# Attention followed by an MLP on one core: scores on half-height row groups side by side, the mask as a factor, two units issued together

## The chip, the cores and the metric

The kernel runs on one core of a Trainium2 chip. The metric is the device time in microseconds (us); for the kernel before, the median of three runs is 324.76 us (324.6 to 324.99). A profiled execution of the same program gives the trace that is read here. The engines are named as in the profile: PE is TensorE (PEld its weight loads), DVE is VectorE, ACT is ScalarE, POOL is GpSimd and SP is SyncE, which here only issues DMAs.

## The reference

The inputs q, k and v have 4 batches, 8 heads, 768 positions and 64 columns per head. The attention is masked by blocks of 32 positions; its output, heads joined to 512 columns, goes through a residual MLP block:

```python
scores = scale * np.matmul(q, k.transpose(0, 1, 3, 2))      # scale = 1/8
mask = np.abs(blk_i - blk_j) <= window                      # blocks of 32, window 1
mask = mask | (blk_i == 0) | (blk_j == 0) | (blk_i == n_blocks - 1) | (blk_j == n_blocks - 1)
...                                                         # and 3 sampled key blocks per query block
scores = np.where(mask, scores, -1000000000.0)
attn = np.exp(scores - max) ; attn = attn / (sum + 1e-09)
x = attn @ v                                                # [4, 768, 512]
a1 = alpha1 * x + beta1
u = x + lam * np.einsum('ts,bsd->btd', w_tok, a1)
out = u + lam * (np.maximum((alpha2 * u + beta2) @ w_ch1, 0.0) @ w_ch2)
```

The mask is the same for all batches and heads. The output is float32.

## The kernel before

**Pairs and units.** The 32 heads are taken as 16 pairs of two heads (`i` from 0 to 15, four pairs per batch). A pair has 12 units `(i, c, j)`: `c` picks one of two halves of 384 queries, `j // 3` the head `w`, and `j % 3` a group `jp` of 256 keys. There are 192 units, and the main loop (line 735) has one step for each of them, and a few more at the end. Positions are laid out so that partition p holds positions 6p to 6p+5; tile `o` of six holds every sixth position.

**A unit.** `emit_qk` (line 310) computes the transposed scores of 256 keys by 384 queries: two matmuls (line 324), one per 128 keys (`jj`), into the two banks of an `sp` tile in PSUM, of which there are two. ScalarE then takes the exponential of both banks in one instruction (line 332) into a tile `eT` in f16. `emit_pv` (line 337) multiplies eT with the values: six matmuls (line 345) per unit, which add up in one `op` tile per `(i, c)`. The values have a column of ones beside them, so the row sums come along. The value matmuls of a unit are issued `LAG` = 2 steps after its scores. With the last of a half, `emit_finish` (lines 360, 362) divides by the sums into `x_sb`, and `emit_a1pp` (lines 376, 377) applies alpha1 and beta1, on POOL for all but the last half of a batch.

**The mask before.** It is added within the score matmul. The contraction has 88 rows: 64 columns of the head and 24 rows that hold, for the queries, which of the 24 blocks a position is in, and for the keys a penalty of -400 (`BIG8`) where the block may not be seen. After the scale of 1/8 and the exponential, such a score leaves nothing.

**How q and k get there.** The loads go over POOL's queue and cast to bf16 (line 111). For pairs 0 to 5, VectorE copies q and k into a joint tile (`emit_lay`, line 126), TensorE transposes (line 267) and VectorE copies out of PSUM into rows 0 to 63 of `qTs`/`kTs` (lines 273, 276). For pairs from 6 (`XP`) on, VectorE copies q and k into the tiles `ql`/`kl`, 128 columns per tile of positions, in which the 24 mask columns already stand (`emit_mask_cols`, line 281, and `emit_mask_spread`, line 290, put them there once); a DMA transpose on SP's queue (`emit_tdma`, line 300) writes `qTs`/`kTs`. These are issued in steps 3 and 4 of the pair before, counted from its first unit.

**What else is in the loop.** The order of the work is written out by hand. For the first steps, `at(s, ...)` puts a piece of work on step s: the copies and transposes of the first pairs, the transposes of w_tok, the loads of the MLP's weights, the first token-mixing jobs. From step 55 (`OPEN`) on, `pour` takes MLP jobs from a queue at a fixed rate of cost per step: `job_tok` (line 485; its result is added on VectorE, lines 500 and 506), the transpose of u (by DMA, line 530, and line 539 on VectorE, or on TensorE, lines 515 and 516), `job_f1` (line 553, with the Relu on ScalarE, line 560) and `job_f2` (line 572, with the residual sum on VectorE, line 581, and the store on SP's queue). What is left of the queue after the last unit runs to the end without attention work. Line 453 multiplies w_ch2 by lam once, at steps 64 to 73. The jobs share three PSUM tiles `mm`; each is free again when its result has been read.

**Within a step** the order is: scores of the unit, loads, copies and DMA transposes for a later pair, jobs, value matmuls of an earlier unit. Each engine works off its own instructions in this order, and so does each DMA queue.

Of the kernel before, what the change touches and what calls it, by code (L numbers as in the profile page):

```python
# [11 lines left out]
FP = mybir.dt.float32  # L12
F16 = mybir.dt.float16
BF = mybir.dt.bfloat16
I32 = mybir.dt.int32
AF = mybir.ActivationFunctionType
ALU = mybir.AluOpType
# [3 lines left out]
S = 768  # L21
D = 64
BLK = 32
NBLK = S // BLK
NR = 3
DM = 512
P = 128
NT = S // P
NH = 4 * DM // P
QC = 384  # L30
NP = H // 2
XP = 6
BIG8 = 400.0
SCALE = 1.0 / 8.0
EXPB = -0.35667494
# [6 lines left out]
def kernel(  # L42
# [16 lines left out]
    nc = tc.nc  # L59
# [3 lines left out]
    indq_np = (tok[None, :] // BLK == np.arange(NBLK)[:, None]).astype(  # L63
        ml_dtypes.bfloat16
    )
# [9 lines left out]
    ms_np = np.concatenate([mstat_np] + [kbi_np] * NR, axis=1)  # L75

    ident_dr = nc.inline_tensor(np.eye(P, dtype=ml_dtypes.bfloat16), name="ident_c")
    indt_np = np.ascontiguousarray(
        indq_np.reshape(NBLK, NT, P).transpose(2, 1, 0).reshape(P, NT * NBLK)
    )  # L80
    indt_dr = nc.inline_tensor(indt_np, name="indt_c")
    indq_dr = nc.inline_tensor(indq_np, name="indq_c")
    ident8_dr = nc.inline_tensor(np.eye(8, dtype=np.float32), name="ident8_c")
    ms_dr = nc.inline_tensor(ms_np, name="ms_c")
# [4 lines left out]
    ap_ = ctx.enter_context(tc.tile_pool(name="attn", bufs=1))  # L89
# [4 lines left out]
    def ptile(shape, dt, name):  # L94
        return pp.tile(shape, dt, name=name, tag=name)
# [6 lines left out]
    raws = {}  # L102
    qks = {}

    def emit_load(i, which="qkv"):
        b, hp = i // NP, i % NP
        for nm, src, dt in (("q", q, BF), ("k", k, BF), ("v", v, F16)):
            if nm not in which or (i, nm) in raws:
                continue
            t = ap_.tile([P, 2, NT * D], dt, name=nm + "r", tag=nm + "r", bufs=2)  # L110
            nc.gpsimd.dma_start(  # L111
                t[:], src[b, 2 * hp : 2 * hp + 2].rearrange("w (p o) d -> p w (o d)", o=NT)
            )
            raws[(i, nm)] = t

    def emit_lay(i, nm, w=slice(0, 2), copy=None):
        raw = raws[(i, nm)][:, w].rearrange("p w (o d) -> p w o d", d=D)
        if nm != "v" and i >= XP:
            dst = (qls if nm == "q" else kls)[i % 2][:, w, :, 0:D]
        elif nm == "v":  # L120
            dst = vexts[i % NVB][:, w, :, 0:D]
        else:
            if i not in qks:
                qks[i] = ap_.tile([P, 2, NT, 2, D], BF, name="qk", tag="qk", bufs=2)
            dst = qks[i][:, w, :, "qk".index(nm), :]
        (copy or nc.vector.tensor_copy)(out=dst, in_=raw)  # L126


    for nm in "qkv":
        raws[(0, nm)] = ap_.tile(  # L130
            [P, 2, NT * D], FP, name=nm + "f", tag="otf_" + nm, bufs=1
        )
    sampi = ptile([P, 2 * NR], I32, "sampi")
    ms = ptile([P, (1 + NR) * NBLK], FP, "ms")
    identb = ptile([P, P], BF, "identb")
    NQB = 4
    qTs = [ptile([P, 2, S], BF, f"qTs{i}") for i in range(NQB // 2)]
    kTs = [ptile([P, 2, S], BF, f"kTs{i}") for i in range(NQB // 2)]
    qText = [qTs[n // 2][:, n % 2] for n in range(NQB)]
    kText = [kTs[n // 2][:, n % 2] for n in range(NQB)]  # L140

    qls = [ptile([P, 2, NT, P], BF, f"ql{i}") for i in range(2)]
    kls = [ptile([P, 2, NT, P], BF, f"kl{i}") for i in range(2)]
    indt = ptile([P, NT, NBLK], BF, "indt")
    maskt = ptile([P, NT, NBLK], BF, "maskt")

    def load_first(nm, src, w, eng):
        eng.dma_start(
# [26 lines left out]
        )  # L175
    for i in range(2, NQB):
        nc.sync.dma_start(qText[i][D : D + NBLK, :], indq_dr.ap())
    nc.sync.dma_start(indt[:], indt_dr.ap().rearrange("p (o n) -> p o n", o=NT))
    warm = ptile([P, DM], BF, "warm")
    nc.vector.memset(warm[:], 0.0)  # L180
    for t in vexts:
        nc.gpsimd.memset(t[:, :, :, D : D + 1], 1.0)
    for t in qls + kls:
        nc.gpsimd.memset(t[:, :, :, D + NBLK : P], 0.0)

    gate = ptile([P, 1], FP, "gate")
    nc.gpsimd.tensor_copy(out=gate[:], in_=raws[(0, "v")][:, 0, 0:1])
# [60 lines left out]
    def mm_tile(shape=(P, DM), dt=FP):  # L248
        return psum.tile(list(shape), dt, name="mm", tag="mm", bufs=3)
# [28 lines left out]
            )  # L278
            qa = qb

    def emit_mask_cols():
        tps = mm_tile((P, NT, NBLK), BF)
        rows = slice(D, D + NBLK)
        for o in range(NT):
            nc.tensor.transpose(
                tps[:, o, :], kText[0][rows, ts(o, P)], identb[rows, rows]
            )
        nc.vector.tensor_copy(out=maskt[:], in_=tps[:])

    def emit_mask_spread():  # L290
        for ts_, src in ((qls, indt), (kls, maskt)):
            for t in ts_:
                nc.gpsimd.tensor_copy(
                    out=t[:, :, :, D : D + NBLK],
                    in_=src[:].unsqueeze(1).broadcast_to([P, 2, NT, NBLK]),
                )

    def emit_tdma(i, nm):
        dst, src = ((qTs, qls) if nm == "q" else (kTs, kls))
        nc.sync.dma_start_transpose(  # L300
            out=dst[i % 2][:].rearrange("p w (o t) -> p (w o) t", t=P),
            in_=src[i % 2][:].rearrange("p w o d -> p (w o d)"),
        )

    ets = {}
    ops = {}
# [3 lines left out]
    def emit_qk(i, c, j, spare=0):  # L310
        w, jp = j // 3, j % 3
        n = (2 * i + w) % NQB
        sp = sp_tile()
        for jj in range(2):
            for _ in range(spare if jj else 0):
                nc.tensor.matmul(
                    sp[:, 0, QC:],
                    warm[:, 0:P],
                    warm[:, 0:P],
                    start=False,  # L320
                    stop=True,
                    skip_group_check=True,
                )
            nc.tensor.matmul(  # L324
                sp[:, jj, 0:QC],
                kText[n][0 : D + NBLK, ts(2 * jp + jj, P)],
                qText[n][0 : D + NBLK, ts(c, QC)],
                start=True,
                stop=True,
            )  # L330
        eT = ap_.tile([P, 2, QC], F16, name="eT", tag="eT", bufs=5)
        nc.scalar.activation(  # L332
            eT[:], sp[:, :, 0:QC], AF.Exp, bias=expb[:], scale=SCALE
        )
        ets[(i, c, j)] = eT

    def emit_pv(i, c, j):
        w, jp = j // 3, j % 3
# [330 lines left out]
    def at(s, *fns):  # L669
        slots.setdefault(s, []).extend(fns)  # L670
# [15 lines left out]
    at(6, lambda: emit_bcast(0))  # L686
    at(7, lambda: emit_bcast(1))
    at(8, lambda: emit_bcast(2))
    at(13, emit_mask_cols)
    at(14, emit_columns_use)  # L690
    at(60, emit_lam16)
    at(57, emit_mask_spread)
    for i, where in {
        1: (5, 7, 11, 9, 12),
        2: (16, 17, 18, 21, 23),
        3: (20, 21, 28, 27, 32),
        4: (34, 35, 40, 37, 39),
        5: (41, 42, 45, 47, 51),
    }.items():
        for n, nm in enumerate("qkv"):  # L700
            at(where[n], lambda i=i, nm=nm: emit_lay(i, nm))
        for w in range(2):
            at(where[3 + w], lambda i=i, w=w: emit_tps(i, w))
    for i, nm, s in ((3, "qk", 9), (3, "v", 12), (4, "qkv", 22), (5, "qkv", 33)):
        at(s, lambda i=i, nm=nm: emit_load(i, nm))
    for o in range(NT):
# [25 lines left out]
        for fn in slots.get(s, ()):  # L732
            fn()

    for s in range(len(units) + LAG + 1):
        if s < len(units):
            i, c, j = units[s]
            r = s % 12
            emit_qk(i, c, j, zeros.get(s, 0))
            if r == 2 and i + 2 < NPAIR:  # L740
                emit_load(i + 2)
            if XP <= i + 1 < NPAIR:
                if r in (3, 4):
                    emit_lay(i + 1, "qk"[r - 3])
                    emit_tdma(i + 1, "qk"[r - 3])
                if r == 6:
                    emit_lay(i + 1, "v")
        if s >= OPEN:
            fns(s)
        if s in ready:  # L750
            i = ready.pop(s)
            tok, _ = pair_jobs(i)
            queue[0:2] = tok + [(0.0, lambda i=i: emit_udma(i))] + queue[0:2]
            scales[s + 7] = i
        if s in scales:
            emit_uscale(scales.pop(s))
        if s >= OPEN:
            pour()
        if LAG <= s < len(units) + LAG:


            i, c, j = units[s - LAG]
            if j == 1:
                emit_pv(i, c, 0)
            if j > 0:
                emit_pv(i, c, j)
            if j == NT - 1:
                emit_finish(i, c)
                last = (i % NP, c) == (NP - 1, 1)
                emit_a1pp(i, c, nc.vector if last else nc.gpsimd)  # L770
                if last:
                    phase["first"] = False
                    queue.extend(mlp_jobs(i // NP))
                    left = per_b if i >= NP else 2 * per_b - OPEN
                    state["rate"] = (sum(t[0] for t in queue) + 6.2 - CARRY) / left
                elif c == 1 and i >= NP:
                    ready[s + 5] = i
        if s < OPEN:
            fns(s)
# [33 lines left out]
```

## Time and profile before

| what | value |
| --- | --- |
| median of three runs | 324.76 us |
| profiled execution, first to last instruction | 323.1 us (its page gives no time beyond this span) |
| instructions | 7663 |
| granted TensorE clock | 1.000 |
| PE / DVE / ACT / POOL busy | 98% / 43% / 69% / 31% |
| first score matmul of unit 48 / of unit 60 / of unit 191 | 50.3 / 64.9 / 259.4 us |
| score matmuls (line 324) | 384, mean 326 ns from start to modelled end |
| exponentials (line 332) | 192, mean 901 ns |
| f1 / f2 matmuls (lines 553, 572) | 512 / 368 |
| copies of q / k to ql / kl (line 126) | 10 / 10, mean 378 / 826 ns |
| DMA transposes ql / kl / uraw on SP's queue | 10 / 10 / 11 |

The page of a profile gives the busy time of each engine, then its busy share in 40 equal slices (each digit in tenths), then groups of instructions by line. In a windows answer, each line is a stretch in us with the busy time and number of instructions of PE, PEld, DVE, ACT and POOL, the granted clock, the busy share of the DMA engines and their GB/s. In a timeline, the first two numbers are the start and the length of a group of like instructions in us, and `x6` their number. A matmul's end is modelled and overlaps the start of the next, so TensorE's pace is read from start to start: 0.16 us for 384 columns, 0.22 us for 512.

### The profile page before, as it was taken

The page shows a single profiled execution, that of the slowest core. Times are in us where ns is not written, and L with a number is a line of the kernel's source. Part 1 is how long each engine was busy: PE and PEld are TensorE (multiplying, and loading weights), DVE is VectorE, ACT ScalarE, POOL GpSimd, SP SyncE. Part 2 cuts the span into 40 slices and gives each one's busy share as a digit, 9 for nine tenths or more (in the row PEclk, how much of TensorE's full clock was granted, in tenths as well). Part 3 has the DMA queues.
Part 4 walks back from the last instruction along what each step waited for, and adds up shares of the span by engine and source line. Part 5 has one row for each costly group of instructions (what it writes and reads, how often), then busy time and mean ns, then how long its engine had stood idle before and what let it go on. Part 6 is the DMA issues. An engine that isn't in the chain of part 4 may idle for free.

```text
span 323.1 us, 7663 instructions
## 1 busy us (share of the span) xinstructions
PE 315.6 (98%) x3216; PEld 205.7 (64%) x3216; DVE 140.0 (43%) x289; ACT 223.2 (69%) x328; POOL 99.0 (31%) x128
## 2 busy tenths in 40 slices
PE   8889999999999999999999999999999999999996
PEld 3667878667675766676665756676665756555543
DVE  4889988557343345331534444242332434000011
ACT  4889998998878776878768675678877740553310
POOL 7566746443434411132525402142222200000000
PEclk9999999999999999999999999999999999999999
DMA  6999996969392976091665966097430011000012
GB/s 168 197 191 164 143 156 110 165 114 140 57 177 54 169 120 131 32 172 27 127 103 96 138 106 128 34 155 74 108 52 32 15 46 65 32 34 32 32 43 89
DMA packets 61898, 32.56 MB, mean 101 GB/s; under 512 B 42000, under 2 KB 58756, under 8 KB 61736
## 3 DMA queue, kind: packets, MB, share of 16 engines
q0 software_dynamic: 16608, 14.22, 31.2%
q1 hardware_dynamic: 44680, 17.23, 25.2%
q10 hardware_dynamic: 576, 0.62, 0.7%
q8 instruction: 25, 0.41, 0.5%
q14 instruction: 9, 0.07, 0.1%
HBM read 29.97 MB, written 6.29 MB: 112 GB/s over the span
## 4 chain that ended last, share of the span: by engine, by line
PE 90%; DVE 7%; POOL 1%; issue 1%; ACT 1%; DVEq 0%; POOLq 0%
PE mm L553 26%; PE mm L572 25%; PE sp L324 16%; PE mm L485 10%; PE op L345 9%; PE op L260 1%; PE mm L592 1%; DVE qTs L276 1%; DVE wtokT L469 1%; DVE kTs L273 1%; PE mm L267 1%; DVE qk L126 1%; DVE x_sb L362 1%; POOL a1pp L376 1%; POOL a1pp L377 1%
## 5 line engine op out<-in xcount | busy, mean ns | idle before, releaser
L332 ACT ACTIVATE eT<-sp,expb 128x768 f16<-128x768 f32 x192 | 170.4, 901 | 47.3 <-PE sp L324 44.6
L553 PE MATMUL mm<-uT,w1b 128*128 128x384 bf16 x512 | 100.1, 325 | 0.0
L324 PE MATMUL sp<-qTs,kTs 88*128 88x384 bf16 x384 | 95.5, 326 | 0.9 <-ACT eT L332 0.5
L572 PE MATMUL mm<-w2b,hts 128*128 128x512 bf16 x368 | 92.3, 379 | 0.0
L560 ACT ACTIVATE hts<-mm 128x384 bf16<-128x384 f32 x128 | 61.8, 488 | 35.4 <-PE mm L553 35.0
L376 POOL TENSOR_TENSOR a1pp<-x_sb,vbc 128x384 bf16<-128x384 f32 x28 | 28.3, 1009 | 150.7 <-DVE x_sb L362 150.7
L553 PEld LDWEIGHTS <-w1b 128*128 128x128 bf16 x512 | 49.3, 97 | 36.1 <-issue 0.9
L345 PEld LDWEIGHTS <-eT 128*128 128x128 f16 x1152 | 55.9, 97 | 21.9
L572 PEld LDWEIGHTS <-hts 128*128 128x128 bf16 x368 | 35.3, 97 | 33.9
L345 PE MATMUL op<-vext,eT 128*128 128x65 f16 x1008 | 53.8, 193 | 0.0
L581 DVE TENSOR_TENSOR ot<-x_sb,mm 128x512 f32<-128x512 f32 x23 | 15.8, 686 | 66.9 <-PE mm L572 66.9
L485 PE MATMUL mm<-a1pp,wtokT 128*128 128x128 bf16 x576 | 41.6, 219 | 0.9 <-DVE qTs L276 0.3
L485 PEld LDWEIGHTS <-wtokT 128*128 128x128 bf16 x576 | 35.6, 97 | 6.6 <-PE mm L345 0.4
L500 DVE TENSOR_TENSOR x_sb<-x_sb,mm 128x384 f32<-128x384 f32 x32 | 17.6, 550 | 49.3 <-PE mm L485 48.5
L324 PEld LDWEIGHTS <-kTs 88*128 88x128 bf16 x384 | 28.3, 98 | 6.9 <-issue 1.4
L377 POOL TENSOR_TENSOR a1pp<-a1pp,vbc 128x384 bf16<-128x384 bf16 x28 | 26.7, 952 | 2.2
L506 DVE CAST ubf<-x_sb 128x384 bf16<-128x384 f32 x32 | 17.7, 553 | 1.1
L360 DVE RECIPROCAL rcp<-op 128x6 f32<-128x6 f32 x28 | 5.3, 191 | 29.5 <-PE op L345 29.2
L362 DVE TENSOR_TENSOR x_sb<-op,rcp 128x384 f32<-128x384 f32 x28 | 15.6, 558 | 1.0
L539 DVE TENSOR_SCALAR uT<-uraw,ab2T 128x768 bf16<-128x768 bf16 x11 | 5.4, 493 | 16.8 <-DMA uraw<-ubf 16.8
L111 POOL DMA_DIRECT2D qr<-in_q_dram x15 | 11.4, 761 | 3.1 <-DVE qk L126 3.1
L111 POOL DMA_DIRECT2D kr<-in_k_dram x15 | 10.8, 721 | 0.9 <-DVE qk L126 0.9
(74 smaller groups left out, 147.4 us busy)
## 6 DMA issues: line engine op xcount, KB each, us to landing
out_dram<-ot SPq DMA_DIRECT2D x23, 256.0 KB
qr<-in_q_dram POOLq DMA_DIRECT2D x15, 192.0 KB, 4.6
kr<-in_k_dram POOLq DMA_DIRECT2D x15, 192.0 KB, 6.3
vr<-in_v_dram POOLq DMA_DIRECT2D x15, 192.0 KB, 6.8
w1b<-in_moe_w_ch_dram POOLq DMA_DIRECT2D x4, 512.0 KB, 6.4
w2b<-in_moe_w_ch_dram POOLq DMA_DIRECT2D x4, 512.0 KB, 6.7
hts<-in_moe_w_tok_dram POOLq DMA_DIRECT2D x1, 1152.0 KB, 11.2
kf<-in_k_dram ACTq DMA_DIRECT2D x2, 192.0 KB
```

The costliest lines, as they stand in the source:

```text
L111: nc.gpsimd.dma_start(t[:], src[b, 2 * hp : 2 * hp + 2].rearrange("w (p o) d -> p w (o d)", o=NT))
L324: nc.tensor.matmul(sp[:, jj, 0:QC], kText[n][0 : D + NBLK, ts(2 * jp + jj, P)], qText[n][0 : D + NBLK, ts(c, QC)], start=True, stop=True,)
L332: nc.scalar.activation(eT[:], sp[:, :, 0:QC], AF.Exp, bias=expb[:], scale=SCALE)
L345: nc.tensor.matmul(op[:, w, o, :], eT[:, jj, ts(o, P)], vexts[i % NVB][:, w, 2 * jp + jj, :], start=(j == 0 and jj == 0 and o == 0), stop= ...
L362: nc.vector.tensor_tensor(out=x_sbs[b][:, ts(c, 3), cols].rearrange("p o (w d) -> p w o d", w=2), in0=op[:, :, :, 0:D], in1=rcp[:].unsquee ...
L376: eng.tensor_tensor(out=dst, in0=x_sbs[b][:, sl, cols], in1=bc[0], op=ALU.mult)
L377: eng.tensor_tensor(out=dst, in0=dst, in1=bc[1], op=ALU.add)
L485: nc.tensor.matmul(ps[:, o % 3, :], wtokT[:, os_, ts(o, P)], a1pps[i][:, os_, :], start=(os_ == 0 and o % 3 == 0), stop=(os_ == NT - 1 and ...
L506: nc.vector.tensor_copy(out=ubfs[i][:, sl, :], in_=x_sbs[b][:, sl, ts(hp, P)])
L553: nc.tensor.matmul(ps[:, 0:QC], w1b[:, dk, ts(n, P)], uTs[b][:, dk, ts(c, QC)], start=(dk == 0), stop=(dk == 3),)
L560: nc.scalar.activation(hts[(b, c)][:, n, :], ps[:, 0:QC], AF.Relu)
L572: nc.tensor.matmul(ps[:], ht[:, nk, ts(o % 3, P)], w2b[:, nk, :], start=(nk == 0), stop=(nk == NH - 1),)
```

## The change

For pairs from 4 (`MP`) to 15, which are 144 of the 192 units, the scores are computed in another way; pairs 0 to 3 stay as they were.

- **Scores.** The contraction has 64 rows, without the mask. The 64 columns of a head fill only half of TensorE's rows, so the raw q and k, in which two 64-column tiles of positions lie side by side in 128 columns, are transposed as they are: `khT` has the even tiles of positions in rows 0 to 63 and the odd ones in rows 64 to 127. The two matmuls of a unit (`jj` 0 and 1) take the lower and the upper rows. The queries are needed in both halves: `qhT` holds them twice, shifted by one tile of positions, so that any three tiles follow each other in each half. The exponential has no mask in it any more.
- **Mask.** `emit_mask01` makes a tile `mask01` of zeros and ones for all keys and queries once, in steps 19 to 49: twelve matmuls over the 24 mask rows, each followed by a comparison on VectorE out of PSUM. `emit_keep` multiplies each `eT` in place by its part of `mask01` on VectorE, one step after the unit's scores.
- **Order.** The scores of two units are issued together at each even step. The value matmuls come three steps after a unit instead of two, and there are six `eT` buffers instead of five.
- **Transposes.** From pair 6 on, DMA transposes read the raw tiles: one of six 128x128 blocks for k, two (six and seven blocks) for q, which is loaded into a padded tile `qpad` for that. VectorE's copies of q and k fall away. For pairs 4 and 5, `emit_tph` transposes the raw tiles on TensorE, with one copy for k and three for q.
- **The rest.** `ql`, `kl`, `indt`, `maskt` and what fills them are gone; the first pair's float32 inputs are put into a buffer of `x_sb`.

```diff
+MP = NP
...
+QS = 2 * NT + 1
...
+            if nm == "q":
+                t = qpads[i % 2][:, D : D + 2 * NT * D].rearrange(
+                    "p (w x) -> p w x", w=2
+                )
...
-        if nm != "v" and i >= XP:
-            dst = (qls if nm == "q" else kls)[i % 2][:, w, :, 0:D]
-        elif nm == "v":
+        if nm == "v":
...
+    def emit_mask01(o, c):
+        rows = slice(D, D + NBLK)
+        ps = mm_tile()
+        nc.tensor.matmul(
+            ps[:, 0:QC],
+            kText[0][rows, ts(o, P)],
+            qText[0][rows, ts(c, QC)],
+            start=True,
+            stop=True,
+        )
+        nc.vector.tensor_scalar(
+            out=mask01[:, o, ts(c, QC)],
+            in0=ps[:, 0:QC],
+            scalar1=-BIG8 / 2,
+            scalar2=None,
+            op0=ALU.is_ge,
+        )
+
+    def emit_tph(i, nm):
+        raw = raws[(i, nm)].rearrange("p w (m y) -> p (w m) y", y=P)
+        tps = mm_tile((P, NT, P), BF)
+        for m in range(NT):
+            nc.tensor.transpose(tps[:, m, :], raw[:, m], identb[:])
+        if nm == "k":
+            nc.vector.tensor_copy(out=khTs[i % 2][:], in_=tps[:])
+            return
+        dst = qhTs[i % 2]
+        nc.vector.tensor_copy(out=dst[:, 1 : QS - 1 : 2], in_=tps[:])
+        nc.vector.tensor_copy(out=dst[0:D, 2:QS:2], in_=tps[D:P])
+        nc.vector.tensor_copy(out=dst[D:P, 0 : QS - 1 : 2], in_=tps[0:D])
 
     def emit_tdma(i, nm):
-        dst, src = ((qTs, qls) if nm == "q" else (kTs, kls))
+        if nm == "k":
+            nc.sync.dma_start_transpose(
+                out=khTs[i % 2][:], in_=raws[(i, nm)].rearrange("p w x -> p (w x)")
+            )
+            return
+        dst, src = qhTs[i % 2], qpads[i % 2]
         nc.sync.dma_start_transpose(
-            out=dst[i % 2][:].rearrange("p w (o t) -> p (w o) t", t=P),
-            in_=src[i % 2][:].rearrange("p w o d -> p (w o d)"),
-        )
+            out=dst[:, 1 : QS - 1 : 2], in_=src[:, D : D + 2 * NT * D]
+        )
+        nc.sync.dma_start_transpose(out=dst[:, 0:QS:2], in_=src[:])
...
-        for jj in range(2):
+        for jj in range(2) if i >= MP else ():
+            rows = slice(D * jj, D * jj + D)
+            lo = NT * w + 3 * c + 1 - jj
+            nc.tensor.matmul(
+                sp[:, jj, 0:QC],
+                khTs[i % 2][rows, j],
+                qhTs[i % 2][rows, lo : lo + 3],
+                start=True,
+                stop=True,
+            )
+        for jj in range(2) if i < MP else ():
...
-        eT = ap_.tile([P, 2, QC], F16, name="eT", tag="eT", bufs=5)
+        eT = ap_.tile([P, 2, QC], F16, name="eT", tag="eT", bufs=6)
...
+    def emit_keep(i, c, j):
+        if i >= MP:
+            eT, jp = ets[(i, c, j)], j % 3
+            nc.vector.tensor_mul(
+                out=eT[:], in0=eT[:], in1=mask01[:, 2 * jp : 2 * jp + 2, ts(c, QC)]
+            )
...
-    at(13, emit_mask_cols)
...
-    at(57, emit_mask_spread)
...
-        4: (34, 35, 40, 37, 39),
-        5: (41, 42, 45, 47, 51),
...
+    for i, sv, sk, sq in ((4, 40, 37, 39), (5, 45, 47, 51)):
+        at(sv, lambda i=i: emit_lay(i, "v"))
+        at(sk, lambda i=i: emit_tph(i, "k"))
+        at(sq, lambda i=i: emit_tph(i, "q"))
+    for n, s in enumerate((19, 21, 23, 25, 27, 29, 31, 32, 37, 39, 48, 49)):
+        at(s, lambda n=n: emit_mask01(n // 2, n % 2))
...
+    pvs = {}
+    for u, (i, _, _) in enumerate(units):
+        pvs.setdefault(u + LAG + (i >= MP), []).append(u)
+
+    for s in range(len(units) + LAG + 2):
+        if s == len(units):
+            emit_keep(*units[s - 1])
...
-            emit_qk(i, c, j, zeros.get(s, 0))
+            if i < MP:
+                emit_qk(i, c, j, zeros.get(s, 0))
+            elif s % 2 == 0:
+                emit_qk(i, c, j)
+                emit_qk(*units[s + 1])
+            if s > 0:
+                emit_keep(*units[s - 1])
...
-                    emit_lay(i + 1, "qk"[r - 3])
                     emit_tdma(i + 1, "qk"[r - 3])
...
-            i, c, j = units[s - LAG]
+        for u in pvs.get(s, ()):
+            i, c, j = units[u]
```

## The prediction

> **What bounds the kernel now.** I read the busy shares first, then the stage windows, then the timeline where the new operations have relatives. In the page's parts 1 and 2:
>
> ```profile
> PE 315.6 (98%) x3216; PEld 205.7 (64%) x3216; DVE 140.0 (43%) x289; ACT 223.2 (69%) x328; POOL 99.0 (31%) x128
> PE   8889999999999999999999999999999999999996
> DVE  4889988557343345331534444242332434000011
> ACT  4889998998878776878768675678877740553310
> ```
>
> TensorE is busy throughout, but the first 60 us are also full on VectorE and ScalarE. The windows (PE, weight loads, DVE, ACT, POOL) say where:
>
> ```profile
> 20.00:25.00 5.00, 4.19 (x66) 3.45 (x66) 4.37 (x12) 4.19 (x6) 4.46 (x6) 1.00 1.09 167
> 25.00:30.00 5.00, 4.57 (x72) 3.71 (x70) 4.58 (x12) 4.55 (x6) 3.49 (x6) 1.00 1.10 169
> 45.00:50.00 5.00, 4.92 (x81) 4.12 (x81) 3.46 (x10) 4.83 (x6) 2.21 (x4) 1.00 0.66 113
> 50.00:55.00 5.00, 4.66 (x78) 3.85 (x75) 4.79 (x11) 4.38 (x6) 4.09 (x6) 1.00 0.74 118
> 55.00:60.00 5.00, 4.99 (x66) 3.70 (x65) 4.13 (x10) 4.46 (x8) 0.00 (x0) 1.00 1.22 191
> ```
>
> VectorE is at 83 to 96% just where masks (20 to 52 us) and the first multiplications (from 50 us) are put. From 80 to 260 us it is at 67.8 of 180 us, ScalarE at 70 to 80%, and only TensorE sets the pace. There a unit looks like this, and the timeline also has the one run of matmuls on few rows:
>
> ```profile
> 18.94 0.35 PE L345 MATMUL mm<-vext,eT 128*128 128x65 f16 x6
> 19.22 0.31 PE L285 MATMUL mm<-identb,kTs 24*128 24x24 bf16 x6
> 19.46 0.34 PE L324 MATMUL sp<-qTs,kTs 88*128 88x384 bf16 x1
> 19.63 0.33 PE L316 MATMUL sp<-warm 128*128 128x128 bf16 x3
> ...
> 150.48 0.35 PE L345 MATMUL op<-vext,eT 128*128 128x65 f16 x6
> 150.67 0.49 PE L324 MATMUL sp<-qTs,kTs 88*128 88x384 bf16 x2
> 151.00 0.81 PE L553 MATMUL mm<-uT,w1b 128*128 128x384 bf16 x4
> ```
>
> Two score matmuls occupy TensorE from 150.67 to 151.00, 0.163 us each. Six value matmuls (L345) step by 0.03. At 19 us that rhythm breaks. The last L345 starts at 18.94+0.35-0.193 (its mean duration)=19.10, and the 24-row L285 only at 19.22: 0.12, 0.09 more than a step. The last L285 starts at 19.22+0.31-0.168=19.36, the next full-height matmul at 19.46: 0.10 where L285 steps by 0.03, and that first one takes 0.17 instead of 0.16. Neither start has an engine to wait for in the trace. So one excursion to a short row group and back costs about 0.18 us.
>
> For the new VectorE work:
>
> ```profile
> 69.02 1.16 DVE L126 COPY kl<-kr 128x768 bf16<-128x768 bf16 x1
> 70.10 1.94 DVE L453 TENSOR_TENSOR w2b<-w2b,lam_bcb 128x2048 bf16<-128x2048 bf16 x1
> 72.49 1.20 DVE L453 TENSOR_TENSOR w2b<-w2b,lam_bcb 128x2048 bf16<-128x2048 bf16 x1
> 119.77 0.35 DVE L126 COPY kl<-kr 128x768 bf16<-128x768 bf16 x1
> ```
>
> The same copy takes 0.35 or 1.16, the same product 1.20 or 1.94. The long ones overlap POOL's L376/L377.
>
> **The change part by part.** Sums are against the profiled execution, span 323.1 us; its page gives no time beyond the span. The median of the runs, 324.76, is 1.7 more, which I keep as constant.
>
> *Scores, TensorE.* A group of two units is four matmuls, 4 x 0.163 = 0.65 us now. It becomes two side-by-side pairs plus one excursion, since all else on the engine is full height. If the halves overlap, a pair lasts one matmul; the second half starts one weight-load step later, 0.03 us by L345. Group: 2 x 0.163 + 0.03 + 0.18 = 0.535, a gain of 0.115. No row shows two row groups at once, so the bounds are: halves in series, 0.65 + 0.18 = 0.83 (0.18 lost); no excursion cost, 0.355 (0.295 gained). I take overlap, since the halves use disjoint rows and different PSUM banks, and the excursion at its row. The Trainium skill, "TensorE: Matmul & The Clock Gate", Part 3, says that matmuls on distinct row groups run concurrently, starting about 4 ns apart. By that the group would be 0.51, and the forecast below about 326.5 instead of 328.2; no run here shows it yet. Of 72 groups, ten (units 48 to 67, 50 to 69 us) lie where ScalarE or VectorE sets the pace and count nothing; 62 x 0.115 = -7.1 us.
>
> *Issued together, ScalarE.* With two sp buffers, the second unit of a group needs the exp of the previous second unit. From the first score to the exp's start is 0.59 us now (scores at 153.85, exp at 154.44, ScalarE idle before), some 0.46 with overlap. Two exps of 0.9 end 2.25 us after the group's start, later by what relu work (0.49 each) is in front. Groups now last 2.3 to 3.5 us (score starts, unit 60 on), three of 66 under 2.5; in nine ScalarE's own work is longer than the group. Bounds 0 and 3 (nine groups by a third); I take +1.
>
> *Mask factor, slots 19 to 49.* Twelve 24-row matmuls over 384 columns, each in its own excursion: 12 x (0.163+0.18) = 4.1 us of TensorE, less the six transposes removed (0.3). Twelve VectorE compares out of PSUM at 0.55 (L362, 128x384, 558 ns) = 6.6 us, less q and k copies of pairs 4 and 5 (1.6) and the mask copy (0.2). Ten fall in 20 to 50 us, where VectorE has 25.5 us of work in 30: 25.5+5.5-1.8 = 29.2. TensorE has 1.7 us idle there and gets 3.1. Using all idle time gives +0.7 for all twelve (ScalarE's queue, 26 exps in 22.3 us without a gap, could absorb more); using none, with some VectorE waits, +5. I take +3.
>
> *Multiplications, VectorE.* 144 products of 128x768 f16. L453 undisturbed does 2048 in 1.20 us; taking its step, about 0.45 to 0.5, and with 0.1 fixed 0.55. In-place full rate one per element would be 0.95 (L362 scaled: 768 at about 1.05 ns plus 0.15), the upper bound. Between 50 and 60 us some nine fall in: 9 x 0.55 = 5, plus two compares 1.1 and one more q copy 0.55, on 8.9: 15.6 in 10 us. What is queued behind is everything VectorE does for that step (x_sb sums, casts, finish); who waits are the value matmuls, now three units behind instead of two. A first unit's product is done about 2 us after its group starts, its value matmul comes three units, 3.7 us, later: 1.7 to 2 us can be swallowed. +3.5 (bounds 0, if 60 to 70 us, only 3.7 busy, takes it, and 6). Between 70 and 80 us: 8.3 + 7 x 0.6 = 12.5 in 10, minus 2 swallowed: +1 (0 to 2).
>
> *The rest of the way, 80 to 260 us.* VectorE: 67.8 - 10.9 (nine pairs of q and k copies, 0.38 + 0.83) + 114 x 0.55 = 120 us. Then POOL: two L376/L377 instructions of 1 us per six units. By L453's 1.94 and 1.20 a product that meets one gains 0.74; half that on 38 is 14 us: 134 of 180, 74%. That fits, yet the x_sb sums that free mm buffers come late now and then: +2 (0 to 8). The Trainium skill, "SBUF — State Buffer", on the port pair that VectorE and GpSimd share, calls it an exclusive lock: the loser waits for the whole instruction. By that each of the 38 would cost up to a full 1 us, VectorE stand at 88% and this term nearer to 6 than to 2, the time at some 332; the trace agrees on the kl copy (1.16 = 0.35 + most of L376), and less on the product.
>
> *At nothing.* SP issues three transposes per pair (q twice) for two: about 3 x 1.21 (uraw's, same size) instead of 1.43+2.07, without the wait for VectorE's copies, past the output DMAs and uraw on the same queue. A uraw transpose lands 2.8 us after issue (94.99 to 97.76); three take under 9 us, and first use is eight units, 12 us, later. Without that cover each late us would be one per pair, ten in all. POOL loses four memsets and four spreads (1.7 us at 63 us, idle behind) and now waits for transposes before it reloads q and k, done a pair earlier. PE transposes of pairs 4 and 5 stay twelve. The later finish at the end is covered by f2 matmuls (twelve in a row at 264.57 now).
>
> **Sum:** -7.1 + 1 + 3 + 3.5 + 1 + 2 = +3.4: span 326.5, time 328.2.
>
> **The rivals.**
> 1. *Early work is absorbed; faster.* VectorE catches up in its free 60 to 70 us and the masks use idle time: -7.1 + 0.7 + 0 to 3 = 318.4 to 321.5, up to 324 with some waits. For it: PE waits on VectorE hardly at all now. Against: VectorE at 97% with the masks. It decides if the costs of masks and products stay under 7.1.
> 2. *The halves run in series.* The change then doesn't do what it says: 62 x 0.18 = +11.2, plus 3 + 3.5: 342.5. For it: no row with overlap. Against: disjoint rows and banks.
> 3. *VectorE becomes the bound.* Products at 0.95 or each blocked by POOL: 114 x 0.4 = 46 us more, 166 to 180 of 180: about +8 to +14 over no change, 333 to 340.
>
> **How the numbers follow.** The forecast's own range is 325.4 to 333, chance 0.48. Rival 1 (under 324.1) 0.27; within 0.2%, about 0.65 us and what a measurement of this kernel can tell from no change, 0.07, where gain and early costs cancel; rival 2 0.10; rival 3 0.08. The range 318.4 to 340 leaves out rival 2 and the tails of 1 and 3, under 0.2. Faster 0.27, same 0.07, slower 0.66.
>
> **What would show it.** Score matmuls of 64 rows in pairs starting about 0.03 us apart (right) or 0.16 (rival 2); about 0.1 us lost before and after each group of four; unit 48 starting near 53 us instead of 50.3; L345 waiting for VectorE at 50 to 60 us; VectorE near 75% from 80 us; steady groups 0.1 us shorter. I am wrong above all if the excursion costs less when the engine is fed on both sides than at 19 us, or if a product takes 0.9 us.

## The result, and the profile after

The changed kernel takes 328.51 us (median of four runs, 328.39 to 330.13) against 324.68 us before (four runs): a ratio of 1.0127, 95% interval 1.0105 to 1.0149. It is slower by 3.8 us. The profiled execution took 328.59 us, its span is 326.8 us, 3.7 us more than before.

The page of the changed kernel, busy times and the 40 slices, answers to the lines of before:

```profile
PE 313.4 (96%) x3222; PEld 188.3 (58%) x3222; DVE 220.3 (67%) x420; ACT 220.6 (67%) x328; POOL 102.7 (31%) x124
PE   8887999789999999999999999999999999999996
DVE  4898877967998878868678677868677765000011
ACT  5886889659877876687878766688877640543410
PEclk9999999979999999999999999999999999999999
L371 DVE TENSOR_TENSOR eT<-eT,mask 128x768 f16<-128x768 f16 x144 | 96.9, 703 | 13.7 <-ACT eT L363 13.5
```

VectorE has 80 us more to do: 97 us for the 144 products (L371), less the copies that fell away. TensorE's row now dips at the fourth slice (25 to 33 us) and at the eighth and ninth (57 to 74 us), and the granted clock falls below full speed in the ninth.

Where the time went is read from the first score matmul of a unit, in both traces:

| unit | before, us | after, us | late by |
| --- | --- | --- | --- |
| 20 | 25.6 | 25.6 | 0.0 |
| 48 | 50.3 | 55.0 | 4.7 |
| 60 | 64.9 | 74.8 | 10.0 |
| 72 | 81.7 | 91.0 | 9.3 |
| 188 | 254.5 | 257.7 | 3.2 |
| end of span | 323.1 | 326.8 | 3.7 |

So the change loses 10.0 us in 40 units, before and while the new scores begin, and then wins 6.7 us back (9.95 - 3.21) in the 128 units from 60 to 188. The timeline of TensorE in the changed kernel shows what it wins:

```profile
150.54 0.35 PE L383 MATMUL op<-vext,eT 128*128 128x65 f16 x6
150.82 0.50 PE L338 MATMUL sp<-qhT,khT 64*128 64x384 bf16 x4
151.25 1.18 PE L523 MATMUL mm<-a1pp,wtokT 128*128 128x128 bf16 x18
```

Four score matmuls (L338) take the place from 150.82 to 151.25, where four took 0.65 us before. In the trace's single records they start at 150.824, 150.827, 150.997 and 151.000: the two halves run at once, 3 ns apart. The price stands at both ends. The last of the six value matmuls (L383) starts at 150.54+0.35-0.193=150.70, and without a gap the next would follow 0.03 later; 0.09 is lost ahead of the group. Behind it, the last pair's 0.163 would be over at 151.16, and the next matmul starts at 151.25: 0.09 again.

And what it loses, in windows of the changed kernel (PE, weight loads, DVE, ACT, POOL, clock):

```profile
57.00:60.00 3.00, 2.26 (x29) 1.30 (x26) 2.90 (x8) 1.35 (x3) 2.45 (x4) 1.00 1.20 191
60.00:64.00 4.00, 3.30 (x56) 2.41 (x55) 3.94 (x9) 2.71 (x4) 0.00 (x0) 1.00 1.20 189
64.00:67.00 3.00, 1.02 (x10) 0.52 (x8) 2.97 (x8) 1.18 (x2) 0.00 (x0) 1.00 1.27 206
67.00:71.00 4.00, 4.00 (x28) 2.08 (x27) 1.76 (x4) 2.67 (x4) 0.00 (x0) 0.57 0.99 164
```

From 57 to 67 us VectorE (third pair of numbers) is busy for 9.8 of 10 us, and TensorE has work for 6.6. The chain of work that ended last runs through VectorE almost without a break from 56.57 to 66.52 us: masks, products, the copies of q, the x_sb sums and casts. Then the clock is granted at 0.57 on the mean.

### The profile page after: what moved, and what is told of

Its sections match the earlier page's. It is cut to its first block, busy times and chain, and to the rows that moved or that the text cites. A ratio compares the mean times of both kernels' runs of the same rounds, so it can differ in the third digit from the quotient of the medians.

```text
span 326.8 us, 7815 instructions
## 1 busy us (share of the span) xinstructions
PE 313.4 (96%) x3222; PEld 188.3 (58%) x3222; DVE 220.3 (67%) x420; ACT 220.6 (67%) x328; POOL 102.7 (31%) x124
## 4 chain that ended last, share of the span: by engine, by line
PE 82%; DVE 13%; ACT 3%; issue 2%; DVEq 0%; ACTq 0%
PE mm L591 25%; PE mm L610 24%; PE mm L523 9%; PE sp L338 8%; PE op L383 8%; DVE eT L371 3%; ACT eT L363 3%; PE sp L355 3%; DVE w2b L491 1%; DVE qTs L278 1%; PE op L262 1%; PE mm L630 1%; DVE kTs L275 1%; DVE x_sb L400 1%; PE mm L383 1%
## 5 line engine op out<-in xcount | busy, mean ns | idle before, releaser
L363 ACT ACTIVATE eT<-sp,expb 128x768 f16<-128x768 f32 x192 | 162.6, 897 | 37.9 <-PE sp L338 30.0
L371 DVE TENSOR_TENSOR eT<-eT,mask 128x768 f16<-128x768 f16 x144 | 96.9, 703 | 13.7 <-ACT eT L363 13.5
L591 PE MATMUL mm<-uT,w1b 128*128 128x384 bf16 x512 | 101.3, 329 | 1.7 <-DVE uT L577 1.3
L414 POOL TENSOR_TENSOR a1pp<-x_sb,vbc 128x384 bf16<-128x384 f32 x28 | 32.4, 1158 | 151.3 <-DVE x_sb L400 116.7
L383 PEld LDWEIGHTS <-eT 128*128 128x128 f16 x1152 | 55.5, 98 | 24.3 <-issue 1.3
L591 PEld LDWEIGHTS <-w1b 128*128 128x128 bf16 x512 | 44.7, 98 | 39.5 <-issue 14.7
L383 PE MATMUL op<-vext,eT 128*128 128x65 f16 x1008 | 54.1, 194 | 0.6 <-DVE eT L371 0.4
L523 PEld LDWEIGHTS <-wtokT 128*128 128x128 bf16 x576 | 33.0, 98 | 7.2 <-issue 4.9
L338 PE MATMUL sp<-qhT,khT 64*128 64x384 bf16 x288 | 36.4, 330 | 0.3 <-ACT eT L363 0.3
L415 POOL TENSOR_TENSOR a1pp<-a1pp,vbc 128x384 bf16<-128x384 bf16 x28 | 29.1, 1039 | 2.2
L355 PE MATMUL sp<-qTs,kTs 88*128 88x384 bf16 x96 | 24.5, 326 | 1.8 <-ACT eT L363 1.3
L400 DVE TENSOR_TENSOR x_sb<-op,rcp 128x384 f32<-128x384 f32 x28 | 15.6, 558 | 1.0
L338 PEld LDWEIGHTS <-khT 64*128 64x128 bf16 x288 | 8.5, 94 | 11.5 <-issue 8.5
L114 POOL DMA_DIRECT2D qpad<-in_q_dram x15 | 11.4, 762 | 2.8 <-DVE qk L127 2.8
```

The costliest lines, as they stand in the source:

```text
L338: nc.tensor.matmul(sp[:, jj, 0:QC], khTs[i % 2][rows, j], qhTs[i % 2][rows, lo : lo + 3], start=True, stop=True,)
L355: nc.tensor.matmul(sp[:, jj, 0:QC], kText[n][0 : D + NBLK, ts(2 * jp + jj, P)], qText[n][0 : D + NBLK, ts(c, QC)], start=True, stop=True,)
L363: nc.scalar.activation(eT[:], sp[:, :, 0:QC], AF.Exp, bias=expb[:], scale=SCALE)
L371: nc.vector.tensor_mul(out=eT[:], in0=eT[:], in1=mask01[:, 2 * jp : 2 * jp + 2, ts(c, QC)])
L383: nc.tensor.matmul(op[:, w, o, :], eT[:, jj, ts(o, P)], vexts[i % NVB][:, w, 2 * jp + jj, :], start=(j == 0 and jj == 0 and o == 0), stop= ...
L400: nc.vector.tensor_tensor(out=x_sbs[b][:, ts(c, 3), cols].rearrange("p o (w d) -> p w o d", w=2), in0=op[:, :, :, 0:D], in1=rcp[:].unsquee ...
```

## The experiments

Each was compared with the kernel before on the same chip (324.56 to 324.73 us there). The question was which of the terms of the sum made the 3.8 us. "Unit 48 late" and the like are against the profiled execution of the kernel before.

### One unit at a time

```diff
-            elif s % 2 == 0:
-                emit_qk(i, c, j)
-                emit_qk(*units[s + 1])
+            else:
+                emit_qk(i, c, j)
```

> The changed kernel with the scores of each unit issued alone, at its own step; all else is kept. Theory (each short excursion of TensorE to 64 rows costs about 0.18 us, paid once per two units in the changed kernel): twice as many excursions, 72 x 0.18 = 13 us more on TensorE; 66 of these groups lie where TensorE sets the pace, so 338 to 341 us, a group of two units 0.7 us of TensorE, and the stretch from unit 60 to unit 188 longer than in the kernel before (0.05 per two units, +3 us) instead of 6.8 us shorter. Rival (the pairs hurt, because the second unit waits for ScalarE and the excursion is covered in the steady part): 326 to 329 us.

Measured: 340.85 us, ratio 1.0518 (1.0462 to 1.0574). From unit 72 to 188 it needs 177.7 us, where the changed kernel needs 166.7 and the kernel before 172.8: 11.0 us for 58 excursions more, 0.19 us each. The timeline of this run has them around each unit:

```profile
151.66 0.35 PE L383 MATMUL op<-vext,eT 128*128 128x65 f16 x6
151.94 0.34 PE L338 MATMUL sp<-qhT,khT 64*128 64x384 bf16 x2
152.21 0.82 PE L591 MATMUL mm<-uT,w1b 128*128 128x384 bf16 x4
```

From the end of the value matmuls (151.82+0.03) to the next full-height matmul are 0.36 us, more than the 0.33 that two matmuls one after the other take. Issued alone, the side-by-side scores lose; issued in twos, they win 0.105 us per two units (172.8-166.7=6.1 over 58 groups). The theory stands; the stretch from 60 to 188 became 5.5 us longer than before, not 3.

### No products

```diff
     def emit_keep(i, c, j):
-        if i >= MP:
+        if i >= 99:
```

> The changed kernel without the multiplication by the mask (pairs 4 to 15 see all blocks; the mask is still built). Theory (the products cost only where VectorE was full already, units 48 to 60, where 5.3 us were lost): units 48 to 60 lose 1 us or less, unit 60 to 188 stays as in the changed kernel within 1 us, 322 to 324.5 us in all. Rival (the products also slow the steady part through late PSUM buffers, some 2 to 4 us, as the prediction had it): 318 to 321 us.

Measured: 324.06 us, ratio 0.9985 (0.9975 to 0.9994). Units 48 to 60 lose 1.6 us instead of 5.3, more than the 1 us expected, so 3.7 us of the 5.3 go with the products. Some 1.7 of these are not the products themselves but the half clock that follows them in the changed kernel (last section); it does not occur there without products. What makes the remaining 1.6 was not taken apart: the last two masks and the copies of q also stand there, and the kernel with the new scores from pair 6 on (below), which has these masks but not these copies, loses 1.5. This profiled execution is not the usual one: its clock was at half speed from 31.7 to 35.1 us, unit 48 is late by 6.0 us in it, and it took 325.21 us, the nine others 323.77 to 324.35. From 60 to 188 it takes 181.9 us against 182.8 with the products. In windows, the two kernels' VectorE over the long middle part, first without products:

```profile
80.00:260.00 180.00, 179.53 (x1957) 106.37 (x1956) 63.46 (x127) 139.14 (x206) 55.85 (x63) 1.00 0.52 89
```

then the changed kernel:

```profile
80.00:260.00 180.00, 178.96 (x1953) 106.11 (x1950) 141.77 (x251) 138.52 (x206) 60.38 (x62) 1.00 0.53 88
```

78 us more VectorE work, from 35 to 79% busy, cost 0.9 us there. The rival, that products slow the steady part by 2 to 4 us, falls.

### No building of the mask

```diff
+    at(40, lambda: nc.gpsimd.memset(mask01[:], 1.0))
...
-        at(s, lambda n=n: emit_mask01(n // 2, n % 2))
```

> The changed kernel with the mask tile filled with ones by POOL at step 40, in place of the twelve 24-row matmuls and twelve comparisons; the products stay (pairs 4 to 15 see all blocks). Theory (the 4.7 us lost before unit 48 are the mask's): unit 48 at 50 to 51 us instead of 55.0, the loss between units 48 and 60 somewhat less than 5.3 since two of the twelve lie there, 322 to 324 us in all. Rival (the new transposes of pairs 4 and 5 with their four copies are what costs): unit 48 at 53 us or later.

Measured: 323.29 us, ratio 0.9949 (0.9931 to 0.9967). Unit 48 starts at 50.4 us: all 4.7 us ahead of it are the mask's, and the new transposes of pairs 4 and 5 cost nothing there. Over the whole time the mask costs 5.2 us: the two executions with a mean granted clock of 0.995 took 323.3 us, the three of the changed kernel with the same clock 328.4 to 328.6. The second half of the expectation missed: units 48 to 60 lose 6.1 us, not less than 5.3, with TensorE's clock at half speed for 6.8 us from 60.6 us on, twice as long as in the changed kernel.

### What of the mask it is

Five runs took the mask's cost apart. The first had the matmuls at full height, so that TensorE makes no excursion for them:

```diff
+    nc.vector.memset(indz[0:D, :], 0.0)
+    nc.sync.dma_start(indz[D : D + NBLK, :], indq_dr.ap())
...
-        rows = slice(D, D + NBLK)
+        rows = slice(0, D + NBLK)
...
-            qText[0][rows, ts(c, QC)],
+            indz[rows, ts(c, QC)],
```

> The changed kernel with the twelve mask matmuls at full height: the moving operand is a tile with zeros in rows 0 to 63 and the block indicators in rows 64 to 87, so TensorE makes no excursion to 24 rows for them; the comparisons and their steps stay. Theory A (the excursions are most of the mask's 4.7 us): ten excursions of 0.18 us less before unit 48, so it starts 1.8 us or more earlier, at 53 us or before, 326 to 327 us in all. Theory B (what costs is that a mask matmul and its comparison take one of the three PSUM tiles in VectorE's order, and TensorE waits for VectorE): unit 48 at 54 to 56 us, 327 to 329 us.

Measured: 327.17 us, ratio 1.0079 (1.0064 to 1.0094); unit 48 late by 4.5 us. The excursions alone were not it, as theory B had it. Most of the 1.3 us that it is faster than the changed kernel come later: its clock did not fall in any of the four executions, and units 48 to 60 lose 3.6 us instead of 5.3. The second had no comparisons: emit_mask01 ends after the matmul, and the tile is filled with ones as above.

> The changed kernel with the twelve 24-row mask matmuls but without the comparisons; the mask tile is filled with ones by POOL at step 40 (pairs 4 to 15 see all blocks). Theory A (TensorE's part, 12 x 0.34 us, is most of the 4.7 us): unit 48 at 53 to 54 us. Theory B (VectorE's part and the PSUM tiles that wait for it): unit 48 at 50.3 to 52 us, since the ten matmuls before it (3.4 us with their excursions) find 1.7 us of idle TensorE and wait for nothing behind them. In all 323 to 326 us.

Measured: 326.88 us, ratio 1.0060 (1.0040 to 1.0081); unit 48 late by 5.2 us, outside both theories, as is the time. The lateness cannot be read cleanly, since its profile has the clock at half speed for 3.4 us from 33.0 us on. Whole times of equal granted clock, 0.995, say a little more: 327.44 us in one execution here, 328.4 to 328.6 with the comparisons, so in this order they account for about 1 us. Its timeline shows a wait that the comparisons have no part in, 1.22 us before the mask's matmul at 30.91 us. The changed kernel has the same one, shown here:

```profile
29.78 0.50 PE L269 MATMUL mm<-identb,qk 128*128 128x128 bf16 x6
30.32 0.56 DVE L275 COPY kTs<-mm 64x768 bf16<-64x768 bf16 x1 [0.80 <-PE mm L269]
30.89 0.55 DVE L278 COPY qTs<-mm 64x768 bf16<-64x768 bf16 x1
31.50 0.33 PE L286 MATMUL mm<-qTs,kTs 24*128 24x384 bf16 x1 [1.22 <-DVE qTs L278]
```

The mask's matmul (L286) stands right behind a transpose (L269) and waits until VectorE has copied that transpose out (L275, L278). A reading that fits is that the PSUM tile it needs is the transpose's own, the other mm tiles being held by sums; which tile it got was not shown. Six of the ten masks ahead of unit 48 stood behind such a transpose in the changed kernel (steps 21, 23, 27, 32, 37 and 39; the expectation below says seven); two of them waited, this one and one for 0.21 us. The third run moved them:

```diff
-    for n, s in enumerate((19, 21, 23, 25, 27, 29, 31, 32, 37, 39, 48, 49)):
+    for n, s in enumerate((17, 18, 19, 20, 25, 26, 29, 30, 34, 35, 42, 44)):
```

> The changed kernel with the twelve mask matmuls and comparisons at steps 17, 18, 19, 20, 25, 26, 29, 30, 34, 35, 42 and 44, none of which also has a transpose of q and k; before, seven of the ten that lie ahead of unit 48 stood in the same step behind such a transpose. All twelve are now ahead of unit 48; the amount of work on each engine is the same. Theory (a mask matmul behind a transpose waits until VectorE has copied that transpose out, since the other PSUM tiles of the ring are held by running sums; the two runs without excursions and without comparisons kept the loss because they kept this order): unit 48 late by 1 to 3 us instead of 4.7, no wait of TensorE over 1 us for VectorE between 20 and 50 us, 325 to 327.5 us. Rival (the work is too much for the crowded stretch wherever it is put): unit 48 late by 4 us or more, 327.5 to 330 us.

Measured: 327.35 us, ratio 1.0079 (1.0061 to 1.0097). The long waits are gone as expected, and the time is in the theory's range, but unit 48 is late by 4.4 us, now with all twelve masks ahead of it: there the rival was right. The order is not free of transposes either: steps 17 to 20 have those of w_tok, and unit 20 is late by 1.0 us, where the changed kernel has it on time. The fourth joined both edits:

> Both edits at once: mask matmuls at full height (no excursions) and at the steps without a transpose. Theory (two causes that hide each other: behind a transpose the wait for its copies swallows the excursion, so taking the excursion alone away gained nothing before unit 48, and at steps without that wait the excursions, 12 x 0.18 = 2.2 us, are paid in full): unit 48 late by 12 x 0.163 = 2.0 us and at most 1 us more, so by 2 to 3 us, instead of 4.4 to 4.7 with either edit alone; 325 to 326 us. Rival (the comparisons on VectorE are what costs, whatever TensorE does): unit 48 late by 4 us or more.

Measured: 326.92 us, ratio 1.0048 (1.0028 to 1.0067); unit 48 late by 3.6 us, between the two expectations, and the time above the expected one. The last took the comparisons out of that kernel:

> The kernel with full-height mask matmuls at the steps without a transpose, but without the twelve comparisons on VectorE; the mask tile is filled with ones by POOL at step 40 (pairs 4 to 15 see all blocks). That kernel has unit 48 late by 3.6 us, of which 2.0 are the matmuls' own time. Theory (the other 1.6 are VectorE's: 6.6 us more work where it is 90% busy): unit 48 late by 1.7 to 2.4 us. Rival (VectorE has no part, the extra matmuls only upset the order of TensorE and ScalarE): unit 48 late by 3.2 us or more.

Measured: 325.26 us, ratio 1.0016 (1.0005 to 1.0026); unit 48 late by 1.2 us, less than the theory's 1.7 to 2.4. In this order the mask's parts can be read off at unit 48, from one profiled execution each: 1.2 us for twelve matmuls (2.0 us of work, the rest in idle time), 2.4 for the twelve comparisons (3.6-1.2; VectorE is 88% busy from 20 to 50 us with them), 0.8 for the excursions (4.4-3.6). In the whole time 1.7 us of the comparisons (326.92-325.26) and 0.4 of the excursions (327.35-326.92) remain. A reading that fits the order of the change is that the parts hide each other: who waits for a transpose's copies anyway loses nothing by an excursion. How the 4.7 us of that order divide is not settled.

### The new scores from pair 6 on, and the mask later

Both losses arise where work was put into stretches in which VectorE has little room; the mask's also has TensorE's matmuls and excursions in it. Two kernels use the new scores two pairs later; pairs 4 and 5 stay as they were before. The first builds the mask at the same steps:

```diff
-MP = NP
+MP = 6
...
+        4: (34, 35, 40, 37, 39),
+        5: (41, 42, 45, 47, 51),
...
-    for i, sv, sk, sq in ((4, 40, 37, 39), (5, 45, 47, 51)):
```

> The changed kernel with the new scores from pair 6 on instead of pair 4; pairs 4 and 5 are as in the kernel before (copies, joint transposes, mask within the matmul), the mask tile is built at the same steps. Theory (products from unit 72 on meet a VectorE that has room): unit 48 still about 4.5 us late, units 48 to 72 lose 0 to 1.5 us, the rest gains 0.106 per two units, 58 x 0.106 = 6.1 us: 323 to 325 us, the same as the kernel before. Rival (the loss at units 48 to 60 is only moved to 72 to 84, where the w_ch2 products are): 327 to 329 us.

Measured: 325.64 us, ratio 1.0042 (1.0026 to 1.0057), somewhat above the expected range. Unit 48 is late by 5.2 us, units 48 to 72 lose 1.6, the rest wins 6.8. The products that begin at unit 72 meet w_ch2's products and cost nothing visible: units 72 to 84 take 15.6 us, 16.4 before. The second also moves the mask to steps 57 to 69 and has its matmuls at full height:

```diff
-    for n, s in enumerate((19, 21, 23, 25, 27, 29, 31, 32, 37, 39, 48, 49)):
-        at(s, lambda n=n: emit_mask01(n // 2, n % 2))
+    for n, s in enumerate((57, 58, 59, 60, 61, 62, 63, 64, 65, 66, 68, 69)):
+        at(s, lambda n=n: emit_mask01(n % NT, n // NT))
```

> The new scores from pair 6 on, the mask built at full height in steps 57 to 69, one matmul and comparison each, after the crowded first 55 us and before the first product at step 73. Theory (the early losses come from putting masks and products where VectorE is full; the gain per group is 0.106 us): unit 48 at 50.3 us, units 48 to 72 lose 0 to 2 us (twelve matmuls of 0.163 us where ScalarE has no room either), the rest gains 58 x 0.106 = 6.1 us: 318.5 to 320.5 us, faster than both. Rival (the steady gain needs the late start, because work was put off to it): 322 to 325 us.

Measured: 321.1 us, ratio 0.9890 (0.9875 to 0.9905): faster than both, and between the two expectations. Unit 48 is on time (0.3 us early), units 48 to 72 lose 2.3 us, units 72 to 188 win 6.7 (the changed kernel 6.1 there; the difference is not explained), and the end of the span is 3.8 us early. Its windows show VectorE with room where the masks now are:

```profile
40.00:60.00 20.00, 19.21 (x287) 15.19 (x285) 16.56 (x37) 18.64 (x24) 9.34 (x12) 1.00 1.00 143
60.00:80.00 20.00, 19.89 (x205) 13.46 (x204) 12.80 (x26) 17.62 (x28) 8.01 (x10) 1.00 0.83 120
```

The same with the mask matmuls on 24 rows:

> The same as the run with the new scores from pair 6 and the mask at steps 57 to 69, but with the mask matmuls on 24 rows as in the changed kernel, so twelve excursions more. Excursions at 0.18 us each on a busy TensorE: 2.2 us slower than that run, 320.5 to 322.5 us. Rival (there ScalarE sets the pace, so TensorE's excursions are free): within 0.7 us of it.

Measured: 322.49 us, ratio 0.9934 (0.9919 to 0.9948). Units 48 to 72 lose 4.5 us instead of 2.3: 2.2 us for twelve excursions, 0.18 each, as expected. In the whole time 1.4 us of it remain, since unit 48 is 0.4 us earlier here and the stretch behind unit 188 0.4 us shorter.

## Why the prediction was right

The direction and the time (328.2 for 328.51) came out, and the main mechanism did: a gain on TensorE in the steady part, eaten by work put into the full first 65 us. That the sum is off by no more than 0.3 us is luck: two groups of its terms were off by 3.5 and 3.2 us, in opposite directions.

- *Scores.* Forecast: 0.535 us per group, 0.115 gained, -7.1 in all. Measured: about 0.53 between the value matmuls and the next job, 0.105 gained per group from unit to unit, -6.7 from unit 60 to 188. The excursion, taken from six 24-row transposes at 19 us, was right at 0.18 to 0.19. The Trainium skill, "TensorE: Matmul & The Clock Gate", Part 3, has matmuls on distinct row groups start about 4 ns apart; the trace agrees with 3 ns, and the 0.03 us that the sum took was too much by that. The Trainium skill, "TensorEngine Tiling (Array Packing)", Tiling Modes, says that a change of mode drains the engine; the trace agrees that a change costs time, 0.09 us on each side; the drain itself is not seen in it. Rival 2, halves in series, is out.
- *ScalarE +1, the steady part +2, 70 to 80 us +1.* Of these 4 us 1.2 at most show: new score matmuls waited 0.3 us in all for ScalarE, and without any product units 60 to 188 are faster by 0.9 us. These units win 6.7 us in 64 groups, 0.105 each, with products and w_ch2's products in them. This is the part of the sum that was off most: VectorE's load was about right (79% instead of 74%, a product 0.70 us on the mean: 0.55 undisturbed, and 0.99 to 1.36 in 28 of the 144, each of them beside a POOL product, L414 or L415), but at that load little of it reached TensorE. From 75 us on, the first weights of a unit's value matmuls are loaded 2.75 us after its product in the median, and only once did the matmuls wait for a product, 0.45 us at 93.7 us. Rival 3, VectorE as the bound, is out.
- *Mask +3.* Measured 4.7 at unit 48 for ten of the twelve, and 5.2 in the whole time for all, just over the upper bound of 5. One line was misread on the way, without consequence: from 45 to 50 us VectorE is 69% busy (3.46 of 5), not 83 to 96%.
- *Multiplications at 50 to 60 us +3.5.* Units 48 to 60 lost 5.3 us, of which 3.7 go with the products: some 2.0 by themselves, and 1.7 through the half clock. The bounds, 0 to 6, held, but the half clock was in no term; without it the loss there is 3.6 us (mask at full height) or 3.8 (one unit at a time), near the 3.5 forecast.
- *At nothing.* The transposes on SP's queue, the later finish and the transposes of pairs 4 and 5 cost nothing that can be seen: unit 48 without the mask is on time, and the steady groups gain nearly what was forecast. The last stretch, from unit 188 on, is 0.5 us longer (69.14 for 68.66). The value matmuls three steps behind and the sixth eT buffer are in every run; what they are worth by themselves was not measured.

Together: 4.70 + 5.25 - 6.74 + 0.48 = 3.69 us. Forecast were 3 + 3.5 = 6.5 for the early losses, which came to 9.95, and -3.1 for the rest, which came to -6.26.

Rival 1, the early work absorbed, is what the kernel from pair 6 on with the late mask comes to (321.1 us); in the changed kernel the early losses are 10.0 us, well over the 7.1 from which the rival decided.

## What to carry to other kernels

Half-height matmuls side by side halve their time, but each visit between full-height work costs about 0.19 us, so gather enough of them per visit: here two matmuls are a loss and four a gain of 0.105 us. Work that is moved to another engine should be priced in the stage where it lands: the products cost 0.9 us in 128 units at 79% load, and 3.7 us, half clock included, in twelve units where the engine was already full. Starting the new form two pairs later and building the mask at full height behind the crowded stretch gives up some 1.3 us of gain (an estimate: 12 groups of 0.105) and makes unit 72 late by 2.0 us instead of 9.3.

## What was not expected of the hardware

The clock of TensorE fell to half although no single wait was long. In the changed kernel the profile has TensorE waiting 0.97, 0.69 and 1.28 us for VectorE between 59 and 67 us, with matmuls in between, and the clock was then at half speed for 3.41 us, from 67.28 to 70.69 us; at most 1.7 us of work was lost by that. Its timeline at the three waits:

```profile
60.59 0.50 PE L305 MATMUL mm<-identb,qpad 128*128 128x128 bf16 x6 [0.97 <-DVE mask L293]
...
63.72 0.36 PE L383 MATMUL op<-vext,eT 128*128 128x65 f16 x6
64.77 0.34 PE L553 MATMUL mm<-identb,ubf 128*128 128x128 bf16 x3 [0.69 <-DVE ubf L544]
64.95 0.33 PE L591 MATMUL mm<-uT,w1b 128*128 128x384 bf16 x1
66.56 1.85 PE L591 MATMUL mm<-uT,w1b 128*128 128x384 bf16 x7 [1.28 <-DVE uT L577]
```

Counted from the pace of the matmuls rather than from their modelled ends, the longest of these gaps, behind the one L591 at 64.95, is 66.56-64.95-0.16=1.45 us. The Trainium skill, "TensorE: Matmul & The Clock Gate", Part 1, has windows of 3413 ns after which an idle engine is clocked at half; the trace agrees on the length and on the half, and shows it with gaps of no more than 1.45 us. A stall can so cost twice: the wait, and the half speed after it.

Waits of these lengths do not always bring it on. The kernel with the full-height mask waits 0.98, 0.69 and 1.28 us at the same place and keeps its clock. There units 48 to 60 lose 3.6 us instead of 5.3; the difference, 1.7 us, is what the fall can cost. The same program can go either way. One stretch of 3.41 us at half lowers an execution's mean clock by 0.005 (3.41 x 0.5 / 325). Of the ten executions of the kernel with both mask edits, six have 0.993 to 0.995 and took 326.9 to 327.3 us, and four have 0.998 to 1.0 and took 325.1 to 325.3. What decides between them was not found.
